# Gate products on VectorE and another layout of the conversion turns in an attention, gating and mixing kernel

## The chip, the cores and the metric

The kernel runs on one core of a Trainium2 chip. A core has TensorE (matmuls; the profile shows its matmuls as PE and its weight loads as PEld), VectorE (DVE), ScalarE (ACT), GpSimd (POOL) and SyncE (SP, which here issues the DMAs). The metric is device microseconds of one execution. All inputs lie in HBM at the start; the host only lays data out.

## The reference

Three layers follow each other, for 8 batches of 576 tokens and 512 channels.

```python
q_s = softmax(q, over the 64 channels of a head); k_s = softmax(k, over the tokens)
x = q_s @ (k_s.T @ v)                          # 8 heads, joined to 512 channels
h = gelu_tanh(x @ w_in)                        # 512 -> 1024
u, v = h[..., :512], h[..., 512:]
v_n = (v - mean(v)) / sqrt(var(v) + 1e-6) * g_ln
v_s = einsum('ts,bsd->btd', w_sg, v_n) + b_sg[None, :, None]
x = x + (u * v_s) @ w_out
u = x + (U, V applied over the tokens: low rank 32)
out = u + relu(u @ w_ch1) @ w_ch2              # 512 -> 2048 -> 512
```

w_in, w_out, U, V, w_ch1 and w_ch2 arrive as 64-bit floats, and the kernel turns them into 32-bit ones itself. Every matmul operand is split into a high and a low part, and three products (high x high, high x low, low x high) make one.

## The kernel before

**First part, batch by batch (b = 0 to 7).** TensorE's program order is written out by hand throughout; in the batches VectorE's is too, while ScalarE, GpSimd and SyncE get theirs from a planner that fills them by its own estimates. For one batch TensorE does, in this order: the v half of the hidden layer (`emit_Vh`, tiles pv, five token tiles t), the u half (`emit_Uh`, pu, four blocks f), the mixing over tokens (`emit_S`, pS, four blocks f), the key-value product of the next batch (pk), the output layer (`emit_y`, py, four column blocks c) with the transposes of the next batch's q between, and the next batch's x (`emit_xT`, px). Transposes of y and the low rank products of a batch lie between the pv tiles of the next one.

In the S stage each block f is treated as follows. VectorE reads the finished pS and makes gt = pS * gl + bb (line 658). A product gt = gt * u follows (the gate product, line 661): on POOL for blocks 0, 1 and 2, on VectorE for block 3, in every batch. `split_G` then has ScalarE copy gt to gh (the high part) and VectorE subtract to give gl (the low part); it is called for block f - 1 after `emit_S` of block f. TensorE's py needs gh and gl of all four blocks. Before the S stage's work VectorE and POOL do the division of the next batch's q by its sums (`q_norm`, tiles qt<-qt,qs): token tiles 0 and 1 on VectorE, 2, 3 and 4 on POOL.

**Conversion turns.** The channel weights w_ch1 and w_ch2 are converted in the shadow of the batches. A list `chan` holds 176 items: for each of 16 sets four Blocks (load 256 columns of 64-bit words, clamp on POOL, exponent on ScalarE, two integer instructions on VectorE at lines 179 and 180) and then seven Factors, of Block sums and differences for a seven-product scheme, numbered a = 4, 1, 5, 2, 6, 7, 3. A Factor's sum (`merge`, tile f<-f,f) is done for a = 5, 6, 7 and 3; then follow a copy on ScalarE and a subtract on POOL (chw), and SyncE stores the result to HBM (wd<-chw). `more(n)` makes n turns; a turn advances this pipeline by one item, each item being loaded, clamped, started, merged, copied, split and stored in turns of its own (a store comes 7 turns after the item is loaded, a split 5). There are 183 turns in all. In `side["add"]` stands which engine does the sums: POOL for all of them in batches 1 to 6; in batch 7 and after it VectorE for a = 5 and 7.

How many turns come where is written in the tuple `spread[b]`: after each tile of pv, each block of pu, each block of pS, and ahead of each block of py. Batches 1 to 6 have 15 turns each, the last 37. Batch 0 converts the other weights.

**Second part, 280 steps.** After the batches, tokens are taken in five groups (512, 512, 512, 384, 384 columns). A group has 56 steps: 28 that make hidden tiles h from the input u (r = 0 to 27, matmuls mm<-uh,wu and mm<-ul,wu; for the first seven the tile is called pm), then 28 that make the output (mm<-oh,wu and mm<-ol,wu). A step uses one weight tile wu, fetched from wd by SyncE into a ring of five. The first seven steps lie in the last batch, with `more` between them; `u_first` (prep) makes their operands on ScalarE and VectorE in the last batch's u and S stages. From step 7 on the order on ScalarE, VectorE, POOL and SyncE is written by hand too. In each step SyncE's fetch comes first, then the turns that are left, then `h_prep` (oh and ol three steps ahead, by ScalarE and VectorE), VectorE's sums of h (h<-h,h), POOL's sums of the next group's operand (`u_sum`, ust<-ust), and then the matmuls and what VectorE and ScalarE do with the result. The next operand's four loads (ust<-u2d, 512 KB each) are issued in step r = 7. In the first group, where POOL is busy with turns, the four `u_sum`s come at r = 29, 31, 33 and 35 (line 910); in the other groups at 12, 14, 16 and 18. When the last turn is made, the staging memory is closed and the memory for oh and ol opened in its place.

```python
tt(pool if f < NF - 1 else dve, gt, gt, u_t[b][:, f], ALU.mult)      # line 661
add = side["add"][self.a in (6, 3)]                                  # line 344
more(min(left(), 3 - (s % 4 == 0)))                                  # line 1348
```

Of the kernel before, what the change touches and what calls it, by code (L numbers as in the profile page):

```python
# [12 lines left out]
ALU = mybir.AluOpType  # L13
# [9 lines left out]
def fused_kernel(tc, q, k, v, w_in, g_ln, w_sgT, b_sg, w_out, U, V, w_ch1, w_ch2, outT):  # L23
    nc = tc.nc
    B, S, C = q.shape
# [6 lines left out]
    NF = F // P  # L32
# [9 lines left out]
    ORDER = (1, 2, 6, 7, 5, 4, 3)  # L42
# [8 lines left out]
    def tt(eng, out, a, b, op):  # L51
        return eng.tensor_tensor(out=out, in0=a, in1=b, op=op)  # L52
# [246 lines left out]
            cols = slice(h * HS, (h + 1) * HS)  # L299
            yield ConvV(V[:, cols], lambda o=v_w[:, cols]: o, eng)  # L300

    side = {"add": (pool, pool), "low": pool}
    chw = [((stgp, 4),), 0]

    class Block(Conv):
# [23 lines left out]
    class Factor(Block):  # L329
# [11 lines left out]

        def merge(self):
            w = self.keep
            add = side["add"][self.a in (6, 3)]
            if self.a == 5:
                tt(add, w[22], w[21], w[22], ALU.add)
            elif self.a == 6:
                tt(add, w[22], w[22], w[11], ALU.subtract)
            elif self.a == 7:
                tt(add, w[21], w[11], w[21], ALU.subtract)  # L350
            elif self.a == 3:
                tt(add, w[12], w[12], w[22], ALU.subtract)
            self.t = w[{1: 11, 2: 12, 3: 12, 4: 22, 5: 22, 6: 22, 7: 21}[self.a]]
# [110 lines left out]
    def q_norm(b, t, eng=pool):  # L464
        n = TR[t]
        tt(eng, q3(t), q3(t), q_s[b][0:n, t].unsqueeze(2).to_broadcast([n, H, D]), ALU.mult)
# [161 lines left out]
    u_t = {}  # L628
# [13 lines left out]
    def emit_S(b, f):  # L642
        if f == 0:
            g_t[b] = (
                wrk.tile([P, NF, S], F32R, tag="xgh", name="gh"),
                wrk.tile([P, NF, S], F32R, tag="xgl", name="gl2"),
            )
        pS = ps2.tile([P, 2, 512], F32, tag="big", name="pS")
        fs = slice(f * P, (f + 1) * P)
        for t in range(NT):  # L650
            h, l = vh[b, t]
            prod(pS, h[:, fs], l[:, fs], sg_h[:, t], sg_l[:, t], t == 0, False)
        e = vh[b, NT]
        for i, w in enumerate((sg_a, sg_b)):
            for j in range(2):
                mm(pS[:, j, 0:HS], e[:, fs], w[:, j * HS : (j + 1) * HS], False, i == 1)
        gt = tmpp.tile([P, S], F32, tag="gt", name="gt")
        dve.scalar_tensor_tensor(
            out=two(gt), in0=halves(pS), scalar=gl[:, f : f + 1], in1=two(bb), op0=ALU.mult, op1=ALU.add
        )  # L660
        tt(pool if f < NF - 1 else dve, gt, gt, u_t[b][:, f], ALU.mult)
        g_t[b, f] = gt

    def split_G(b, f):
# [237 lines left out]
    def u_side(g, r):  # L902

        n = GROUPS[g]
        if r == 7:
            us[0] = p2["ust"].tile([P, 2, 2, 2, NM], F32, tag="ust", name="ust")
            for h in range(2):
                for j in range(2):
                    u_fetch(g, h, j)
        x = r - 17 * (g == 1)  # L910
        if x in U_SUMS:
            u_sum(U_SUMS[x], n)
        r -= half_steps
        if r in U_HIGH:
            a = U_HIGH[r]
            uc[g, a] = [u_tile(x, a) for x in ("uh", "ul")]
            copy(uc[g, a][0][:, :, 0:n], u_at(*U_AT[a], n))
        if r in U_LOW:
            a = U_LOW[r]
            hi, lo = (x[:, :, 0:n] for x in uc[g, a])  # L920
            low(dve, lo, u_at(*U_AT[a], n), hi)
            if a in (6, 4, 5):
                sent.append(lambda: u_fetch(g, *U_AT[a]))
# [134 lines left out]
    def left():  # L1058
        return len(chan) + LATER[0][1] - at[0]
# [37 lines left out]

    RING = 5
    OPS = 4
    mid = ((0, 0, 0, 0, 0), (0, 0, 0, 0), (0, 2, 3, 3), (3, 3, 1, 0))  # L1100
    spread = [mid] * B
    spread[0] = ((2, 2, 1, 1, 1), (2, 1, 2, 1), (2, 2, 2, 1), (1, 1, 1, 0))
    spread[B - 1] = ((2, 2, 2, 2, 2), (3, 2, 2, 2), (2, 2, 2, 1), (3, 3, 3, 2))
    pieces.extend(conv_w_in(F, pool))
    pieces.extend(conv_w_in(F + CW, pool))
    pieces.extend(conv_w_in(0, pool))
# [65 lines left out]
    for b in range(B):  # L1172
# [37 lines left out]
        if nxt:  # L1210
            k_max(nxt)
        else:
            side["add"] = (dve, pool)
            close_wiv()
            closers = []

            def pool2(key, *args, **kw):
                p2[key], close = opened(key, *args, **kw)
                closers.append(close)

            pool2("uc", side="right")
            prep = u_first()
# [22 lines left out]
        if nxt:  # L1245
            for t in range(NT + 1):
                q_exp(nxt, t)
            k_exp(nxt)
            for t in range(NT + 1):
                q_sum(nxt, t)  # L1250
            q_total(nxt)
            for t in range(NT + 1):
                q_norm(nxt, t, dve if t < 2 else pool)

        if not nxt:
            close_wiu()
# [43 lines left out]
        else:  # L1300
            close_wo()

            def step(s):
                fetch(s + RING)
                products(s)
                after(s)
                more((1, 1, 1, 1, 2, 2, 2)[s])

            step(0)
            step(1)  # L1310
# [32 lines left out]
    for s in range(len(ORDER), len(steps)):  # L1343
# [1 line left out]
        r = s - g * PER  # L1345
        fetch(s + RING)
        if left():
            more(min(left(), 3 - (s % 4 == 0)))
            if not left():
                close_stgp()  # L1350
                close_cst()
                pool2("ops", side="left")
# [61 lines left out]
```

## Time and profile before

| | us |
|---|---|
| median of 3 runs | 1360.58 |
| lowest and highest | 1359.35, 1360.96 |
| the profiled execution's own time | 1359.37 |
| its span | 1357.6 |
| PE busy | 1278.7 (94%) |
| DVE busy | 993.0 (73%) |
| ACT busy | 663.3 (49%) |
| POOL busy | 433.6 (32%) |

The span is the time from the first instruction to the last. A share of busy time is a mean over parts with different limits, so the rows below are read by stretch. The granted clock (PEclk) is a share of TensorE's 2.4 GHz; over the span it was 0.986.

### The profile page before, as it was taken

Reading aid. Unit: us, or ns where it says so; the run is one execution under the profiler, and the core shown is the slowest. Engines: PE = TensorE matmul, PEld = TensorE weight load, DVE = VectorE, ACT = ScalarE, POOL = GpSimd, SP = SyncE. Lnnn points to the kernel's source line nnn. Section 1 sums busy time; section 2 is a strip of 40 time slices with the busy share of each in tenths; the row PEclk is TensorE's granted clock in tenths of the full one; section 3 lists DMA queues with packets and bytes.
Section 4 is the critical chain, followed back from the end, with each engine's and each line's share of the span. In section 5 each row is a group of like instructions: output and inputs, shape, how many; then the busy total and the mean of one; then the engine's idle time right before and its main releaser. Section 6 shows DMA issues by size and latency. Waiting matters only on the chain.

```text
span 1357.6 us, 20699 instructions
## 1 busy us (share of the span) xinstructions
PE 1278.7 (94%) x7576; PEld 1140.9 (84%) x7576; DVE 993.0 (73%) x1376; ACT 663.3 (49%) x1001; POOL 433.6 (32%) x505
## 2 busy tenths in 40 slices
PE   4579999989999999998998999999999999999998
PEld 2478898979898988887776888888888889999998
DVE  7867868877787777579768974489546974695585
ACT  3774657566666656564445442345224432352342
POOL 4945364663545564466355001100020002000000
PEclk9889999999999999998999999999999999999999
DMA  7513334360616171266897687668776789889786
GB/s 237 164 48 97 105 107 127 110 194 31 178 55 177 60 229 36 94 198 232 294 409 271 220 289 268 197 218 286 242 244 204 242 273 307 264 300 325 258 282 221
DMA packets 136213, 274.68 MB, mean 202 GB/s; under 512 B 15280, under 2 KB 56752, under 8 KB 136112
## 3 DMA queue, kind: packets, MB, share of 16 engines
q1 hardware_dynamic: 136112, 273.37, 60.9%
q8 instruction: 60, 0.98, 0.3%
q14 instruction: 41, 0.34, 0.1%
HBM read 225.09 MB, written 48.23 MB: 201 GB/s over the span
## 4 chain that ended last, share of the span: by engine, by line
PE 68%; DVE 12%; DMA 7%; ACT 6%; issue 3%; POOL 3%; SPq 1%; DVEq 0%; ACTq 0%; POOLq 0%
PE mm L49 46%; PE py L49 5%; PE pu L49 4%; PE pS L49 4%; PE pv L49 3%; DMA wu<-wd 3%; DMA wd<-chw 2%; DVE f L179 1%; DVE km L52 1%; DVE yt L52 1%; DVE bst L603 1%; PE pm L49 1%; PE pt L520 1%; PE px L49 1%; DVE ul L52 1%
## 5 line engine op out<-in xcount | busy, mean ns | idle before, releaser
L49 PE MATMUL mm<-oh,wu 128*128 128x512 f32 (+1 forms) x1120 | 321.8, 368 | 1.7 <-ACT oh L58 1.7
L49 PE MATMUL mm<-uh,wu 128*128 128x512 f32 (+1 forms) x1064 | 305.1, 368 | 5.1 <-DMA wu<-wd 3.6
L49 PEld LDWEIGHTS mm<-oh,wu 128*128 128x128 f32 x1120 | 207.6, 188 | 28.4 <-ACT oh L58 2.2
L49 PEld LDWEIGHTS mm<-uh,wu 128*128 128x128 f32 x1064 | 196.6, 188 | 31.8 <-issue 4.1
L49 PE MATMUL mm<-ol,wu 128*128 128x512 f32 (+1 forms) x560 | 206.6, 369 | 2.5 <-DVE ol L52 2.5
L49 PE MATMUL mm<-ul,wu 128*128 128x512 f32 (+1 forms) x532 | 195.4, 367 | 0.0
L58 ACT ACTIVATE oh<-h 128x1024 fp32r<-128x1024 f32 (+1 forms) x140 | 132.8, 971 | 103.9 <-PE mm L49 99.4
L52 DVE TENSOR_TENSOR ol<-h,oh 128x1024 fp32r<-128x1024 f32 (+1 forms) x140 | 158.0, 1128 | 27.1 <-ACT oh L58 27.0
L1004 ACT ACTIVATE h<-h 128x1024 f32<-128x1024 f32 (+1 forms) x80 | 77.7, 972 | 174.2 <-DVE h L52 174.2
L52 POOL TENSOR_TENSOR ust<-ust 128x1024 f32<-128x1024 f32 (+1 forms) x16 | 35.7, 2239 | 391.7 <-DMA ust<-u2d 250.4
L52 DVE TENSOR_TENSOR h<-mm,u 128x1024 f32<-128x1024 f32 (+1 forms) x76 | 84.4, 1110 | 100.3 <-PE mm L49 97.1
L49 PEld LDWEIGHTS mm<-ol,wu 128*128 128x128 f32 x560 | 105.5, 188 | 17.4 <-DVE ol L52 4.2
L49 PEld LDWEIGHTS mm<-ul,wu 128*128 128x128 f32 x532 | 100.2, 188 | 12.3
L52 POOL TENSOR_TENSOR chw<-f,chw 128x256 fp32r<-128x256 f32 x112 | 87.0, 791 | 58.6 <-ACT chw L58 58.6
L52 DVE TENSOR_TENSOR u<-mm,u 128x1024 f32<-128x1024 f32 (+1 forms) x72 | 79.8, 1108 | 30.8 <-PE mm L49 30.6
L52 DVE TENSOR_TENSOR h<-h,h 128x1024 f32<-128x1024 f32 (+1 forms) x80 | 91.5, 1144 | 0.9 <-ACT h L1004 0.9
L58 ACT ACTIVATE chw<-f 128x256 fp32r<-128x256 f32 x112 | 42.7, 412 | 73.4 <-DVE f L180 27.2
L58 ACT ACTIVATE u<-mm 128x1024 f32<-128x1024 f32 (+1 forms) x24 | 22.5, 937 | 112.0 <-PE mm L49 84.5
L167 POOL TENSOR_SCALAR stg<-stg 128x256 f32<-128x256 f32 (+2 forms) x91 | 46.4, 513 | 55.4 <-DMA stg<-in_w_ch_dram 32.5
L49 PE MATMUL py<-gh,wo_h 128*128 128x288 f32 x256 | 57.6, 307 | 4.6 <-DVE yt L52 2.0
L49 PE MATMUL py<-gl,wo_h 128*128 128x288 f32 x256 | 55.8, 300 | 5.7 <-DVE gl L52 5.7
L49 PE MATMUL pu<-xh,wih 128*128 128x288 f32 x256 | 57.7, 308 | 2.2 <-DVE ge L52 1.5
(162 smaller groups left out, 2692.3 us busy)
## 6 DMA issues: line engine op xcount, KB each, us to landing
wu<-wd SPq DMA_DIRECT2D x280, 512.0 KB, 4.4
wd<-chw SPq DMA_DIRECT2D x112, 256.0 KB, 3.9
stg<-in_w_ch_dram SPq DMA_DIRECT2D x64, 256.0 KB, 3.0
u2d<-yt SPq DMA_DIRECT2D x32, 288.0 KB, 2.3
vt<-in_v_dram SPq DMA_DIRECT2D x32, 256.0 KB, 6.5
qt<-in_q_dram SPq DMA_DIRECT2D x7, 1024.0 KB, 6.8
kt<-in_k_dram SPq DMA_DIRECT2D x7, 1024.0 KB, 6.3
ust<-u2d SPq DMA_DIRECT2D x14, 512.0 KB, 6.3
```

Of the source, the lines that this page charges most:

```text
L49: pe.matmul(out, lhsT, rhs, start=first, stop=last)
L52: return eng.tensor_tensor(out=out, in0=a, in1=b, op=op)
L58: return act.activation(out, src, AF.Copy)
L167: eng.tensor_scalar(out=hi, in0=hi, scalar1=F64_MOST, scalar2=-F64_MOST, op0=ALU.min, op1=ALU.max)
L179: dve.tensor_scalar(out=b, in0=b, scalar1=3, scalar2=None, op0=ALU.logical_shift_left)
L520: pe.transpose(pt[:, t * P : t * P + n], qt[0:n, t, c * P : (c + 1) * P], ident[0:n, 0:n])
L603: dve.bn_stats(out=bst[0:n], in_=ge[0:n])
L1004: act.activation(h, h, AF.Relu)
```

## The change

Five edits are made. The gate product is made by VectorE for blocks 0, 1 and 3 in batches 1 to 6 and for all blocks in batch 7; batch 0 keeps its places. The block sum of a = 5 goes to VectorE in all batches. One q_norm tile (t = 1) goes from VectorE to POOL in batches 1 to 6. The four POOL sums for the second group come at r = 21, 23, 25 and 27. And the turns are laid out anew: batches 1 to 6 have 15, 15, 15, 15, 14 and 16 turns, the last 36, the first seven steps 11 instead of 10; the 46 that are left are taken by the tuple FIRST from step 7 on, and end at step 25, where they ended at step 23.

```diff
-    side = {"add": (pool, pool), "low": pool}
+    side = {"add": {5: dve}, "low": pool}
...
-            add = side["add"][self.a in (6, 3)]
+            add = side["add"].get(self.a, pool)
...
-        tt(pool if f < NF - 1 else dve, gt, gt, u_t[b][:, f], ALU.mult)
+        tt(pool if (f < NF - 1 if b == 0 else f == 2 and b < B - 1) else dve, gt, gt, u_t[b][:, f], ALU.mult)
...
-        x = r - 17 * (g == 1)
+        x = r - 9 * (g == 1)
...
-    mid = ((0, 0, 0, 0, 0), (0, 0, 0, 0), (0, 2, 3, 3), (3, 3, 1, 0))
-    spread = [mid] * B
+    vh0, uh0 = (0, 0, 0, 0, 0), (0, 0, 0, 0)
+    spread = [
+        None,
+        ((1, 0, 0, 0, 0), uh0, (0, 2, 3, 2), (2, 4, 1, 0)),
+        (vh0, (1, 0, 0, 0), (0, 2, 3, 3), (3, 2, 1, 0)),
+        (vh0, (0, 0, 1, 0), (0, 2, 3, 3), (2, 3, 1, 0)),
+        (vh0, uh0, (0, 2, 3, 3), (3, 3, 1, 0)),
+        (vh0, (0, 0, 0, 1), (0, 1, 3, 2), (2, 3, 1, 1)),
+        (vh0, (0, 0, 0, 1), (0, 1, 4, 3), (3, 2, 1, 1)),
+        ((2, 2, 2, 3, 2), (3, 1, 1, 3), (2, 1, 2, 0), (4, 3, 3, 2)),
+    ]
+    FIRST = (2, 2, 3, 2, 2, 3, 3, 3, 2, 3, 3, 3, 1, 3, 4, 2, 1, 2, 3, 3)
     spread[0] = ((2, 2, 1, 1, 1), (2, 1, 2, 1), (2, 2, 2, 1), (1, 1, 1, 0))
-    spread[B - 1] = ((2, 2, 2, 2, 2), (3, 2, 2, 2), (2, 2, 2, 1), (3, 3, 3, 2))
...
-            side["add"] = (dve, pool)
+            side["add"] = {5: dve, 7: dve}
...
-                q_norm(nxt, t, dve if t < 2 else pool)
+                q_norm(nxt, t, dve if t < (1 if b else 2) else pool)
...
-                more((1, 1, 1, 1, 2, 2, 2)[s])
+                more((2, 2, 2, 1, 0, 3, 1)[s])
...
-            more(min(left(), 3 - (s % 4 == 0)))
+            x = s - len(ORDER)
+            more(min(left(), FIRST[x] if x < len(FIRST) else 3))
```

## Rows read from the trace of the kernel before

The stretches of rows 1 are batches 1, 2, 5 and 6 (pu to pu), the last y stage, steps 0 to 6, 7 to 12, 13 to 27, 28 to 31, and 24 later steps; behind the engines stand the granted clock, the DMA share and GB/s.

**Rows 1.** Busy time of each engine in stretches: length, then PE, PEld, DVE, ACT, POOL

```profile
153.87:224.01 70.14, 69.79 (x528) 64.61 (x527) 53.75 (x100) 44.13 (x72) 34.62 (x41) 1.00 0.37 114
224.01:299.23 75.22, 71.15 (x529) 64.44 (x528) 58.72 (x104) 47.48 (x83) 44.46 (x54) 1.00 0.43 137
...
441.20:515.22 74.02, 70.58 (x528) 64.48 (x527) 56.91 (x102) 47.22 (x83) 44.21 (x53) 1.00 0.43 135
515.22:587.99 72.77, 70.50 (x526) 63.99 (x524) 49.67 (x97) 45.22 (x75) 38.40 (x46) 1.00 0.25 83
...
617.33:638.63 21.30, 15.58 (x98) 14.76 (x97) 20.95 (x31) 9.04 (x19) 10.90 (x12) 0.84 0.77 265
638.63:666.52 27.89, 25.51 (x124) 20.34 (x122) 22.75 (x35) 13.55 (x26) 11.31 (x16) 1.00 0.81 261
666.52:687.12 20.60, 18.25 (x72) 14.64 (x73) 11.12 (x19) 6.32 (x14) 9.39 (x13) 0.92 1.01 364
687.12:730.84 43.72, 42.06 (x182) 33.45 (x180) 35.39 (x44) 23.87 (x43) 31.41 (x39) 1.00 1.00 378
730.84:749.02 18.18, 13.94 (x50) 9.74 (x49) 16.11 (x14) 6.97 (x7) 4.04 (x2) 0.91 0.47 174
749.02:814.30 65.28, 65.28 (x290) 54.05 (x289) 55.69 (x49) 29.64 (x29) 0.00 (x0) 1.00 0.77 264
```

**Rows 2.** Waits of PE from 140 to 588 us: total, times, longest

```profile
PE pv L49 <- POOL xl L52: 2.8, 3, 1.9
```

**Rows 3.** Timeline of PE, last y stage: start, us, instruction, idle before it

```profile
622.43 0.85 PE L49 MATMUL py<-gl,wo_h 128*128 128x288 f32 x2 [3.55 <-DVE gl L52]
626.34 0.85 PE L49 MATMUL py<-gl,wo_h 128*128 128x288 f32 x2 [2.11 <-DVE gl L52]
```

**Rows 4.** Timeline of PE where step 12 begins

```profile
682.76 0.70 PE L49 MATMUL mm<-uh,wu 128*128 128x512 f32 x2 [2.35 <-DMA wu<-wd]
```

**Rows 5.** Gate products: duration in ns (min, median, max), first and last start

```profile
L52 POOL TENSOR_TENSOR gt<-gt,ut x24: 1412/1427/1933, 102.5 to 619.3; 128x576 f32<-128x576 f32 x24
L52 DVE TENSOR_TENSOR gt<-gt,ut x8: 757/759/1159, 114.9 to 624.5; 128x576 f32<-128x576 f32 x8
```

**Rows 6.** The q_norm of VectorE, same columns

```profile
L52 DVE TENSOR_TENSOR qt<-qt,qs x19: 631/674/896, 24.2 to 534.5; 128x512 f32<-128x512 f32 x18, 64x512 f32<-64x512 f32 x1
```

**Rows 7.** Timeline of POOL, S stage of batch 4

```profile
388.16 4.19 POOL L52 TENSOR_TENSOR qt<-qt,qs 128x512 f32<-128x512 f32 x3 [10.98 <-ACT kt L432]
```

**Rows 8.** Timeline of DVE, S stage of batch 4

```profile
394.49 1.25 DVE L52 TENSOR_TENSOR gl<-gt,gh 128x576 fp32r<-128x576 f32 x1 [1.85 <-ACT gh L58]
```

**Rows 9.** Timeline of POOL at its sums for the second group

```profile
723.31 11.57 POOL L52 TENSOR_TENSOR ust<-ust 128x1024 f32<-128x1024 f32 x4
```

**Rows 10.** Timeline of DVE during these sums and after them

```profile
723.46 3.33 DVE L52 TENSOR_TENSOR h<-h,h 128x1024 f32<-128x1024 f32 x1 [0.89 <-ACT h L1004]
...
729.18 3.44 DVE L52 TENSOR_TENSOR ol<-h,oh 128x1024 fp32r<-128x1024 f32 x1
...
735.93 1.21 DVE L52 TENSOR_TENSOR h<-h,h 128x1024 f32<-128x1024 f32 x1
```

**Rows 11.** Block sums of Factors, columns as in rows 5

```profile
L52 POOL TENSOR_TENSOR f<-f,f x49: 726/737/1239, 190.1 to 720.3; 128x256 f32<-128x256 f32 x49
...
L52 DVE TENSOR_TENSOR f<-f,f x15: 411/497/959, 596.6 to 717.9; 128x256 f32<-128x256 f32 x15
```

**Rows 12.** Timeline of POOL, S stage of the last batch

```profile
610.00 2.51 POOL L52 TENSOR_TENSOR f<-f,f 128x256 f32<-128x256 f32 x2
...
613.62 1.43 POOL L52 TENSOR_TENSOR gt<-gt,ut 128x576 f32<-128x576 f32 x1
```

**Rows 13.** Timeline of DVE, S stage of the last batch

```profile
615.81 1.95 DVE L52 TENSOR_TENSOR gl<-gt,gh 128x576 fp32r<-128x576 f32 x1 [2.74 <-ACT gh L58]
```

**Rows 14.** Timeline of SP, step 7: issues

```profile
671.15 2.32 SPq L889 DMA_DIRECT2D ust<-u2d  x4
673.86 0.98 SPq L761 DMA_DIRECT2D wu<-wd  x2
```

## The prediction

> **What bounds the kernel now.** I read the table of stretches first. A stretch is compared with its kind at full pace, and what it is longer by is all that a change of order can win, because the number of matmuls stays the same. TensorE is busy for all but fractions of a microsecond in the best of the middle batches: batch 1 takes 70.14 us [rows 1]. Batches 2, 5 and 6 take 75.22, 74.02 and 72.77, so 5.1, 3.9 and 2.6 are lost there; batches 3 and 4 lie between, with little to win. The y stage of the last batch is 21.30 long with 15.58 of TensorE, at 0.84 of the clock. In the steps that follow, 24 undisturbed ones take 65.28, so one step is 2.72. Steps 7 to 12 take 20.60 instead of 16.3 (4.3 lost), steps 13 to 27 take 43.72 instead of 40.8 (2.9), steps 28 to 31 take 18.18 instead of 10.9 (7.3) [rows 1]. Steps 0 to 6 with what lies between them are 27.89 with 25.51 of TensorE (2.4). Together with about 8 of the y stage (5.7 of idle, and the halved clock) that is some 36 us that could be won; everything else is TensorE at its pace.
>
> Then the waits, stretch by stretch, for what ends last. In the middle batches it is POOL's low part of x, 2.8 us in 3 waits [rows 2]; the reader is to see that the two long batches are those with 44.46 and 44.21 us of POOL work, against 34.62 in the shortest [rows 1]. In the last y stage TensorE waits 3.55 and 2.11 us for VectorE's gl [rows 3]. At step 12 it is a fetch that lands late [rows 4]; at steps 28 to 31 the high and low operands, which VectorE makes in its order.
>
> **The change part by part.** Durations are those of the profiled execution (1359.37 us; the median of the runs is 1.2 above it), and the sum is made against it.
>
> *Gate products of batches 1 to 6.* Two of the three POOL products (1.427 us each) go to VectorE, where one takes 0.759 [rows 5]; one q_norm goes the other way, 0.674 on VectorE, and 4.19/3 = 1.4 on POOL [rows 6, 7]. On VectorE that adds 2 x 0.759 - 0.674 = 0.8 us a batch. The cover is the wait for gh in the same stage: VectorE stands 1.85 us before the first gl [rows 8], because POOL makes three q_norms before the two gates [rows 7]; with the gate made by VectorE this wait goes, and what is late next is the scalar product of block 2, which VectorE then reaches at about the same time. Without that cover it would be 0.8 x 6 = 5 us later. TensorE has no wait in this stage, so I take 0, between -2 and +5.
>
> Work of two engines on the same memory shows: an h sum of VectorE takes 3.33 us while POOL runs its sums and 1.21 after them [rows 9, 10]. The Trainium skill, SBUF — State Buffer, section Who interferes with whom, says that a VectorE instruction with two SBUF inputs and a GpSimd instruction that reads SBUF exclude each other for a whole instruction. By that rule each moved gate also waits for the q_norm running beside it, so VectorE would be some 1 us later in each of the batches, which speaks against this part; rows 10 agree with the rule.
>
> *POOL's load in those batches.* It loses 2 x 1.427 for gates and 1.3 block sums of 0.737 [rows 5, 11] (16 sets of 11 items; 90 turns in six batches are 8 sets), and gains 1.4: net -2.4 us a batch. Batches 2 and 5 against batch 1 give 4.5 us of length for 9.7 us of POOL [rows 1], 0.46 us for each, so 1.1 us in each of the three long batches: -3.3. Turns: batch 5 has 7 instead of 9 before its first y add, batch 3 has 8; batch 6 has 10. For this I add -1.7, an estimate of a seventh of the 11.6 lost in the three long batches. The block sum adds 0.497 [rows 11] to VectorE 1.3 times a batch, which lies beside TensorE's py. I take -5; the bounds are -10 (nearly all that is lost) and +5 (one more batch like batch 2, since each batch now meets another phase of the 11 items).
>
> *Last batch.* All gates go to VectorE. Now POOL reaches gate 0 at 613.62 only after two block sums that took 2.51 us [rows 12], and VectorE stands 2.74 us for the first gl, which then takes 1.95 [rows 13], while it has the second block's work behind it. After: three products more (2.3 us), less that wait, less one turn ahead of the last gl, and the first gl no longer runs beside POOL's gate (up to 1.2 us). VectorE should reach the last gl 2 to 3 us earlier, and TensorE stands that much less before its 626.34 [rows 3]. With a part of the halved clock that is -3.5; bounds 0 (VectorE fills the time with other work, being busy 20.95 of 21.30 us [rows 1]) and -8.
>
> *Steps 0 to 6.* 11 turns instead of 10, and 6 instead of 3 in the first three steps, where VectorE also owes the y adds. VectorE has 22.75 of 27.89 us to do there [rows 1]. I take +1; bounds -2.4 and +3.
>
> *Steps 7 to 27.* The turns left are 46, as before. They were 3 or 2 a step and ended at step 23; now they are 2 to 4, and end at step 25. In steps 7 to 12 the fetch for step 12 is issued 2.7 us behind four loads of the next operand (671.15) and lands after TensorE has come to it; TensorE waits 2.35 us and then runs at 0.92 of the clock [rows 1, 4, 14]. 11 turns instead of 14 in steps 7 to 11 put fewer loads and stores into SP's queue around these; but the four loads stay. -1, bounds -4.3 and +2. For steps 13 to 27 I take 0, bounds -2.9 and +4: two steps more with conversions, and three POOL sums between them. SP's stores wait for POOL's low parts, and the fetches stand behind the stores.
>
> *The four sums for the second group.* They moved from steps 29 to 35 to steps 21 to 27 in POOL's order. POOL ran them in one piece, 11.57 us from 723.31 [rows 9], as soon as its conversions were done, and in this piece an h sum took 3.33 and an operand's low part 3.44 us instead of 1.21 [rows 10]: 4.35 us on VectorE, just ahead of the operands for steps 28 to 31. Spread over seven steps three of the four come before that; the last can still meet it: 3/4 of 4.35, or 3.3, so -3.5 with what the halved clock (0.91 in that stretch [rows 1]) gives back; bounds -7.3 and 0.
>
> **Sum:** 0 - 5 - 3.5 + 1 - 1 + 0 - 3.5 = -12, so 1347.4 profiled, and 1348.6 for the runs with the 1.2 between them; I say 1348.5.
>
> **Rivals.** *The middle batches give nothing* (1353.5). Their lost time then does not come from POOL's load but from VectorE's order; the turns and the sums that VectorE gets keep it late. For: x's low part is only 2.8 us of the waits [rows 2]; against: the lengths follow POOL's load [rows 1]. Faster still.
>
> *The gains cancel* (1360). VectorE is the bound of the last y stage (20.95 of 21.30), so the gates cost what the wait gives; the sums slow VectorE in steps 21 to 27 as much as they did later. Then the terms of the last batch and of the sums are 0, the middle gives a little, and the first steps take it. For: VectorE's 35.39 of 43.72 us in steps 13 to 27 [rows 1]. Against: that leaves it 8 us of idle time, and 4.35 are disputed.
>
> *Slower* (1367). The three sums at steps 21, 23 and 25 stand in POOL's queue between conversions whose results SP stores; SP holds the fetches of the weights behind these stores. Each sum is 2.9 us; where the fetch lands with nothing to spare, as it did at step 12 [rows 4], TensorE waits for each: 8.7 us, the sums' gain is lost, and the middle batches give nothing: -3.5 + 1 + 8.7 = +6.2. It decides once POOL falls behind its conversions by more than the ring of five weight tiles covers. For: the stores do wait for POOL. Against: POOL is idle 12.3 us of the 43.72 [rows 1], about what the sums take.
>
> **How the numbers follow.** My forecast gets 0.52, the middle giving nothing 0.20, cancelling 0.11, slower 0.17. Faster by over 0.2% (2.7 us, about what a measurement of this kernel can tell from no change) is then 0.72, within it 0.11, slower 0.17. The likeliest case alone reaches from 1338 to 1354. The range goes from 1335 (the middle and the sums near their better bounds) to 1362, past the cancelling case; about 0.1 of the slower case lies beyond, and some of the better one below.
>
> **What would show it.** Batches 2 and 5 nearer 72 us; the wait for gl in the last y stage under 4 us in all, and no idle time of VectorE before the first gl; steps 28 to 31 in 14 to 15 us, with h sums at 1.2 us there; POOL's sums as four pieces between conversions. Wrong would be: fetch waits in steps 21 to 27, batches of 74 us in other places, or a last y stage of 21 us again.

## The result, and the profile after

| | before | after |
|---|---|---|
| median of the runs, us | 1360.77 (4 runs) | 1345.40 (4 runs) |
| lowest and highest | 1359.35, 1361.32 | 1344.43, 1345.79 |
| the profiled execution, us | 1359.37 | 1344.43 |
| its span | 1357.6 | 1342.7 |

The changed kernel is faster: the ratio of the times is 0.989, with a 95% interval from 0.987 to 0.9905. The forecast was 1348.5. Against the profiled execution of before, where the sum was made, it was -12, and -14.9 came.

The table of stretches comes first, cut at the same points of the program as [rows 1]. Length, then busy time of PE, PEld, DVE, ACT and POOL; behind them the granted clock, the DMA share and GB/s. The stretches of the changed kernel are batches 1 to 6 one by one, then steps 0 to 6, 7 to 12, 13 to 27 and 28 to 31.

```profile
153.77:223.92 70.15, 69.80 (x529) 64.60 (x528) 54.76 (x102) 43.91 (x72) 32.70 (x39) 1.00 0.39 114
223.92:294.12 70.20, 69.85 (x529) 64.61 (x528) 58.82 (x106) 44.66 (x74) 38.62 (x43) 1.00 0.41 128
294.12:365.06 70.94, 70.27 (x528) 64.54 (x527) 55.39 (x101) 47.32 (x81) 38.27 (x46) 1.00 0.42 126
365.06:436.83 71.77, 70.50 (x530) 64.51 (x528) 57.55 (x104) 43.87 (x72) 33.62 (x40) 1.00 0.38 116
436.83:507.43 70.60, 70.01 (x527) 64.60 (x527) 57.18 (x104) 44.51 (x74) 36.01 (x42) 1.00 0.40 123
507.43:580.83 73.40, 70.45 (x524) 64.05 (x523) 54.68 (x101) 49.16 (x86) 44.60 (x53) 1.00 0.30 103
...
627.34:654.62 27.28, 25.60 (x123) 20.24 (x121) 24.31 (x39) 13.45 (x26) 12.83 (x19) 1.00 0.83 279
654.62:672.87 18.25, 16.71 (x73) 13.55 (x74) 9.06 (x14) 4.47 (x9) 6.89 (x10) 1.00 1.02 369
672.87:716.90 44.03, 41.62 (x181) 33.55 (x180) 35.72 (x45) 25.40 (x48) 32.28 (x41) 1.00 1.02 380
716.90:734.30 17.40, 13.42 (x49) 9.87 (x48) 13.99 (x13) 6.97 (x7) 4.86 (x2) 0.90 0.61 212
```

The reader is to see that the long batches 2 and 5 [rows 1] are gone (70.20 and 70.60), that batch 6 is the only long one left, and that in the second part only steps 7 to 12 moved by more than a microsecond. Set side by side, with the stages merged where a cut between them falls differently in two profiles:

| stage | before | after | change | forecast |
|---|---|---|---|---|
| batches 1 to 6 | 434.12 | 427.06 | -7.1 | -5 |
| last batch, its pu to step 0 | 50.64 | 46.51 | -4.1 | -3.5 |
| steps 0 to 6 | 27.89 | 27.28 | -0.6 | +1 |
| steps 7 to 12 | 20.60 | 18.25 | -2.4 | -1 |
| steps 13 to 27 | 43.72 | 44.03 | +0.3 | 0 |
| steps 28 to 31 | 18.18 | 17.40 | -0.8 | -3.5 |
| all after step 31 | 608.57 | 608.35 | -0.2 | |

The total is near, but the split is not: the middle gave more and steps 28 to 31 gave nearly nothing. Their 0.8 us is less than the scatter: the kernel before and two others that are as before from step 7 on took 18.18, 16.44 and 17.17 us there, and the changed kernel and five others that are like it from step 7 on took 16.63 to 19.36. The waits of TensorE in the middle (140 to 590 us of the changed kernel; total, times, longest) no longer name POOL, which ended the most waiting in [rows 2]:

```profile
PE pv L49 <- ACT ge L593: 1.8, 6, 0.5
PE pu L49 <- DVE ge L52: 1.4, 1, 1.4
PE pw L49 <- DVE yt L52: 1.0, 1, 1.0
```

In the last y stage of the changed kernel the two waits of [rows 3] are shorter (timeline of PE: start, us, instruction, idle before it),

```profile
612.11 0.53 PE L49 MATMUL py<-gl,wo_h 128*128 128x288 f32 x2 [0.88 <-DVE gl L52]
614.97 0.85 PE L49 MATMUL py<-gl,wo_h 128*128 128x288 f32 x2 [1.79 <-DVE gl L52]
```

and VectorE no longer stands before the first gl, which takes 0.75 us where it took 1.95 after a wait of 2.74 [rows 13] (timeline of DVE, S stage of the last batch):

```profile
600.23 1.12 DVE L52 TENSOR_TENSOR gt<-gt,ut 128x576 f32<-128x576 f32 x1
...
607.22 0.75 DVE L52 TENSOR_TENSOR gl<-gt,gh 128x576 fp32r<-128x576 f32 x1
```

The four sums of POOL come in three pieces in the changed kernel, the last two sums back to back:

```profile
704.96 2.59 POOL L52 TENSOR_TENSOR ust<-ust 128x1024 f32<-128x1024 f32 x1
...
711.28 3.41 POOL L52 TENSOR_TENSOR ust<-ust 128x1024 f32<-128x1024 f32 x1
...
716.05 5.71 POOL L52 TENSOR_TENSOR ust<-ust 128x1024 f32<-128x1024 f32 x2
```

VectorE's low parts and h sums there, two of which took 3.33 and 3.44 us [rows 10], now take 1.74 to 2.07. But a wait stands before one of them (timeline of DVE, changed kernel, up to step 29):

```profile
710.67 1.75 DVE L52 TENSOR_TENSOR h<-h,h 128x1024 f32<-128x1024 f32 x1 [1.71 <-ACT h L1004]
...
715.42 1.74 DVE L52 TENSOR_TENSOR ol<-h,oh 128x1024 fp32r<-128x1024 f32 x1 [0.55 <-POOL chw L52]
...
720.77 2.07 DVE L52 TENSOR_TENSOR ol<-h,oh 128x1024 fp32r<-128x1024 f32 x1 [1.33 <-DMA wu<-wd]
```

TensorE stands for that low part (timeline of PE, changed kernel):

```profile
722.89 0.50 PE L49 MATMUL mm<-ol,wu 128*128 128x512 f32 x1 [2.65 <-DVE ol L52]
```

A low part made from h and oh needs no weight tile, so "wu<-wd" can't be what it waits for. The DMAs that end just before 720.77 are the last two stores of converted weights, issued at 715.42 and 716.11 and landed at 719.83 and 720.45. Whether these are the cause was tried below.

### The profile page after: what moved, and what is told of

Its sections match the earlier page's. It is cut to its first block, busy times and chain, and to the rows that moved or that the text cites. A ratio compares the mean times of both kernels' runs of the same rounds, so it can differ in the third digit from the quotient of the medians.

```text
span 1342.7 us, 20693 instructions
## 1 busy us (share of the span) xinstructions
PE 1274.2 (95%) x7576; PEld 1139.7 (85%) x7576; DVE 1002.7 (75%) x1393; ACT 662.7 (49%) x1001; POOL 420.1 (31%) x488
## 4 chain that ended last, share of the span: by engine, by line
PE 71%; DVE 13%; DMA 6%; ACT 4%; issue 3%; POOL 2%; SPq 1%; DVEq 0%; ACTq 0%; POOLq 0%
PE mm L49 46%; PE pu L49 5%; PE py L49 5%; PE pS L49 5%; PE pv L49 4%; DMA wu<-wd 2%; DVE f L179 1%; PE px L49 1%; DMA qt<-in_q_dram 1%; POOL chw L52 1%; DVE km L52 1%; DVE yt L52 1%; DVE f L180 1%; PE pp L49 1%; PE pt L692 1%
## 5 line engine op out<-in xcount | busy, mean ns | idle before, releaser
L52 POOL TENSOR_TENSOR chw<-f,chw 128x256 fp32r<-128x256 f32 x112 | 91.9, 837 | 50.1 <-ACT chw L58 47.2
```

## Experiments: the middle batches

All are made from the changed kernel unless the text says otherwise, and each was timed beside the kernel before on its chip. The times of the six batches are those of one profile each. How far they can be trusted shows from kernels whose edits leave these batches alone: seven with the batches of the changed kernel took 425.9 to 427.2 us in them, two with those of before 434.1 and 434.2.

**The gates back on POOL** (batches 1 to 6 alone).

```diff
-        tt(pool if (f < NF - 1 if b == 0 else f == 2 and b < B - 1) else dve, gt, gt, u_t[b][:, f], ALU.mult)
+        tt(pool if (f < NF - 1 if b < B - 1 else False) else dve, gt, gt, u_t[b][:, f], ALU.mult)
```

> The changed kernel, with the gate products of blocks 0 and 1 of batches 1 to 6 back on POOL; all else as changed. Theory A (the two long middle batches were set by POOL's load): POOL gets 2.85 us a batch more, so the batches with most POOL work grow by 1 to 2 us each, about 4 us in all: 1349 us. Theory B (the layout of the turns took the time out, the gates were covered): within 1.5 us of the changed kernel's 1345.4, and the lengths of batches 2 and 5 stay near 70.5.

Measured: 1351.24, ratio to the kernel before 0.994 [0.992, 0.995]. The six batches took 432.59, so 5.5 of the 7.1 us are lost again. Its runs reach from 1348.89 to 1353.89 and the profiled one took 1353.32, so the 5.5 may be on the high side. TensorE's waits there have other names than before (waits of PE, 140 to 590 us):

```profile
PE py L49 <- DVE ql L52: 3.3, 2, 2.1
...
PE py L49 <- DVE yt L52: 1.4, 1, 1.4
```

It now waits for VectorE, and VectorE is late because it stands for POOL's gates. Timeline of DVE in the S stage of batch 6, gates on POOL:

```profile
535.50 1.25 DVE L52 TENSOR_TENSOR gl<-gt,gh 128x576 fp32r<-128x576 f32 x1 [3.23 <-ACT gh L58]
```

The same first low part in the changed kernel:

```profile
531.00 0.96 DVE L52 TENSOR_TENSOR gl<-gt,gh 128x576 fp32r<-128x576 f32 x1 [0.56 <-ACT gh L58]
```

So the cover that the prediction named (VectorE's wait for gh) is there, and its removal is worth time on the path, where the prediction had put 0.

**The gates alone**, added to the kernel before.

```diff
-        tt(pool if f < NF - 1 else dve, gt, gt, u_t[b][:, f], ALU.mult)
+        tt(pool if (f < NF - 1 if b in (0, B - 1) else f == 2) else dve, gt, gt, u_t[b][:, f], ALU.mult)
```

> The kernel before, with the gate products of blocks 0 and 1 of batches 1 to 6 alone moved from POOL to VectorE. Theory A: the six batches come from 434.1 to about 429 us, and the kernel to 1354. Rival B (it takes the new layout of the turns as well): under 2 us of gain, 1358.

Measured: 1353.84, ratio 0.9955 [0.994, 0.997]. The six batches took 429.92: 4.2 of the 7.1 us come from this line alone. The wait for POOL's low part of x is shorter too, where it was 2.8 us in [rows 2] (waits of PE, 140 to 590 us, gates alone):

```profile
PE pv L49 <- POOL xl L52: 0.9, 2, 0.5
```

So a part of the 4.2 us is POOL's relief, and not VectorE's wait for POOL's gates.

**The block sum of a = 5 back on POOL** (batches 1 to 6).

```diff
-    side = {"add": {5: dve}, "low": pool}
+    side = {"add": {}, "low": pool}
```

> The changed kernel, with the block sum of a = 5 back on POOL in batches 1 to 6. Theory A with the slope of the prediction (0.46 us of length for 1 us of POOL): POOL gets 1 us a batch, so 1 to 2 us over all, 1347. Theory K (only the wait of VectorE behind POOL's gates counted, and POOL's other load does not): within 1 us of 1345.4, the six batches together at 427 as now.

Measured: 1350.64, ratio 0.9935 [0.992, 0.995]. The six batches took 432.66, so this one edit holds 5.6 us (the profiled execution, 1352.74, was the longest of its runs). The waits of PE for POOL's low part of x come back as in [rows 2]:

```profile
PE pv L49 <- POOL xl L52: 2.2, 3, 1.2
```

The edit moves nine sums between pu of batch 1 and pu of the last (POOL makes 34 there instead of 25), but it moves more than these. The later sums of a set need the one of a = 5. VectorE's order is written by hand, so in the changed kernel that sum of the second set of batch 2 stands at its turn, in the S stage of batch 3 (317.76 us), and three more sums and five splits (chw) come behind it on POOL. With the sum on POOL, the planner ran all of this ahead of its turns, between 268 and 280 us, around the low parts of x (timeline of POOL, x stage of batch 2, sum on POOL):

```profile
274.03 1.43 POOL L52 TENSOR_TENSOR xl<-x,xh 128x576 fp32r<-128x576 f32 x1
275.41 0.75 POOL L52 TENSOR_TENSOR f<-f,f 128x256 f32<-128x256 f32 x1
276.11 1.44 POOL L52 TENSOR_TENSOR xl<-x,xh 128x576 fp32r<-128x576 f32 x1
```

In the changed kernel the two low parts there run in one piece:

```profile
273.30 2.83 POOL L52 TENSOR_TENSOR xl<-x,xh 128x576 fp32r<-128x576 f32 x2 [3.67 <-PE pt L692]
```

Batch 5 shows the same. With the sum on POOL, as before the change, batches 2 and 5 have 14 splits and 8 sums of POOL each; in the changed kernel they have 9 and 3, and batches 3 and 6 go from 7 and 9 splits to 12 and 16. (Batch 6, the one long batch left, has the work that left batch 5.) The 5.6 us lie in these two batches: they take 72.36 and 75.33 us for 70.20 and 70.60, and the other four together 1.3 us less. So what counts is what the sum takes along, and not its own 0.74 us.

**One q_norm tile back on VectorE.**

```diff
-                q_norm(nxt, t, dve if t < (1 if b else 2) else pool)
+                q_norm(nxt, t, dve if t < 2 else pool)
```

> The changed kernel, with the second q_norm tile of batches 1 to 6 back on VectorE. Theory A (POOL's load sets the long batches): POOL is 1.4 us lighter, 1 to 3 us faster over the six batches: 1343 to 1344. Theory L (VectorE's order sets them): VectorE gets 0.7 us a batch in front of the gates, 1 to 3 us slower: 1347 to 1348. Neither: within 1 us.

Measured: 1345.17, ratio 0.9896 [0.988, 0.991], six batches 426.42. No difference from the changed kernel.

**The turns of batches 1 to 6 as they were.**

```diff
+    mid = ((0, 0, 0, 0, 0), (0, 0, 0, 0), (0, 2, 3, 3), (3, 3, 1, 0))
+    spread[1:7] = [mid] * 6
```

> The changed kernel, with the turns of batches 1 to 6 back in the old places (0, 2, 3, 3 in S and 3, 3, 1, 0 ahead of y in every batch, 90 turns in all as before). Theory A (POOL's load): the relief of POOL stays, so at most 2 us come back: 1345 to 1347. Theory B (the layout): most of the 7.1 us that the middle batches lost comes back, batches 2 and 5 near 74 again: 1350 to 1352.

Measured: 1346.96, ratio 0.9905 [0.989, 0.992], six batches 426.64 against 427.06. The new layout of the turns in these batches is worth nothing that can be measured here: beside the gates and the sum, the old one does as well.

The six batches in one row each (same columns as above): before,

```profile
153.87:587.99 434.12, 422.20 (x3160) 386.48 (x3159) 327.34 (x598) 272.46 (x452) 231.44 (x271) 1.00 0.37 116
```

the changed kernel,

```profile
153.77:580.83 427.06, 420.89 (x3159) 386.90 (x3158) 338.40 (x613) 273.44 (x454) 223.80 (x258) 1.00 0.38 118
```

the block sum back on POOL,

```profile
154.37:587.03 432.66, 422.80 (x3159) 386.47 (x3159) 328.95 (x604) 271.60 (x452) 223.77 (x265) 1.00 0.37 116
```

and the gates alone.

```profile
153.59:583.51 429.92, 422.05 (x3160) 386.51 (x3159) 333.64 (x610) 271.96 (x452) 218.50 (x259) 1.00 0.37 117
```

The last two show that the prediction's yardstick, 0.46 us of length for each us of POOL's load, does not hold. With the block sum on POOL its busy time is that of the changed kernel (223.77 and 223.80), and the batches are 5.6 us longer. With the gates alone POOL has the least to do of all four (218.50), and they are 2.9 us longer. What counts is in which batch and in which place of POOL's order the work stands. The two edits aren't additive either: each undone by itself costs most of the gain (5.5 and 5.6, together 11.1 of 7.1), and yet the gates alone give 4.2. With the sum on POOL the q_norm tile and the new turns together cost 2.7 us (432.66 against 429.92), while with the sum on VectorE each of them is worth nothing. Gates on POOL hold VectorE up, the sum on POOL holds x's low part up, and either is enough to make TensorE late.

## Experiments: the last batch

**Its gates alone**, added to the kernel before.

```diff
-        tt(pool if f < NF - 1 else dve, gt, gt, u_t[b][:, f], ALU.mult)
+        tt(pool if f < NF - 1 and b < B - 1 else dve, gt, gt, u_t[b][:, f], ALU.mult)
```

> The kernel before, with the three gate products of the last batch alone moved from POOL to VectorE. Theory E (VectorE's wait for POOL's gates set the last y stage): the two waits for gl shrink from 5.7 to under 3.5 us and the stage from 21.3 to about 18: 3 us faster, 1357.5. Rival F (VectorE is full, and the fewer turns in that stage did it): within 1 us of before, waits for gl still over 5 us.

Measured: 1356.13, ratio 0.998 [0.997, 0.9985]. From pu of the last batch to step 0 it took 49.28 instead of 50.64. VectorE's wait before the first gl is gone, as expected, but TensorE's two waits are as long as in [rows 3] (timeline of PE, gates alone):

```profile
619.46 0.54 PE L49 MATMUL py<-gl,wo_h 128*128 128x288 f32 x2 [3.02 <-DVE gl L52]
623.51 0.85 PE L49 MATMUL py<-gl,wo_h 128*128 128x288 f32 x2 [2.99 <-DVE gl L52]
```

**The last batch's turns as they were**, with the gates of the changed kernel.

```diff
-        ((2, 2, 2, 3, 2), (3, 1, 1, 3), (2, 1, 2, 0), (4, 3, 3, 2)),
+        ((2, 2, 2, 2, 2), (3, 2, 2, 2), (2, 2, 2, 1), (3, 3, 3, 2)),
...
-                more((2, 2, 2, 1, 0, 3, 1)[s])
+                more((1, 1, 1, 1, 2, 2, 2)[s])
```

> The changed kernel, with the last batch's turns back (10, 9, 7, 11 and 10 in the first seven steps, 47 in all as now). Moving the gates alone took only 1.4 us off the S and y stages of the last batch together (50.6 to 49.3), the whole change 4.1 (46.5). Theory G (the turns ahead of the gates hold the rest, since VectorE is full there): these stages come to 48.5 to 49.5, the kernel to about 1348. Rival H (gates and a run's clock made it all): under 47.3, 1345.5.

Measured: 1347.31, ratio 0.991 [0.989, 0.993]; the stage took 47.58, where the kernels with the new layout in this batch take 46.2 to 47.5. The two waits (timeline of PE, old layout in the last batch):

```profile
611.67 0.53 PE L49 MATMUL py<-gl,wo_h 128*128 128x288 f32 x2 [1.45 <-DVE gl L52]
615.72 0.85 PE L49 MATMUL py<-gl,wo_h 128*128 128x288 f32 x2 [2.99 <-DVE gl L52]
```

Turns and gates of the last batch are the same in these two kernels, and still one takes 1.7 us longer than the other; what they enter the stage with differs. So a part of the 4.1 us may be handed on from the batches before; with one profile each, where kernels with the same last batch lie up to 1.3 us apart, that is not shown. The second wait goes with the layout: it is 2.99 us in both kernels with the old one, and 1.71 to 1.79 in the changed kernel and in eight others of this study with the new one (in the ninth, with the middle gates on POOL, TensorE came to it later and waited 0.26). That is 1.2 us of this wait for the layout, most likely for the two turns fewer between the blocks of pS; in the length of the stage the layout is not told apart from the scatter. How the rest of the 4.1 us divides between the gates and what is handed on stays open; the pieces are as small as the scatter between profiles.

## Experiments: steps 7 to 35

**The four sums back at r = 29 to 35.**

```diff
-        x = r - 9 * (g == 1)
+        x = r - 17 * (g == 1)
```

> The changed kernel, with POOL's four sums for the second group back at r = 29 to 35. Theory C (the sums slow VectorE just ahead of steps 28 to 31, as the prediction had it): steps 28 to 31 get 2 to 4 us longer than 17.4, 1348 us. Theory D (steps 28 to 31 wait for the memory under the operands' low parts, which is free only when the last conversion's store has landed): without sums between them the last conversions end some 4 us earlier, the wait of 2.65 us at step 29 goes, and the kernel is as fast as changed or up to 2 us faster: 1343 to 1346.

Measured: 1346.03, ratio 0.990 [0.989, 0.9915]. POOL does the sums in one piece again (710.47, 11.53 us), and VectorE's h sum beside it takes 3.39 us, with the same wait before the low part (timeline of DVE, sums back):

```profile
717.46 2.31 DVE L52 TENSOR_TENSOR ol<-h,oh 128x1024 fp32r<-128x1024 f32 x1 [1.24 <-DMA wu<-wd]
719.70 3.39 DVE L52 TENSOR_TENSOR h<-h,h 128x1024 f32<-128x1024 f32 x1
```

The stretches of steps 7 to 27 and 28 to 31 of this kernel:

```profile
652.25:714.55 62.30, 58.35 (x253) 47.10 (x254) 44.28 (x60) 29.87 (x56) 37.52 (x50) 1.00 1.02 379
714.55:734.86 20.31, 15.15 (x49) 10.92 (x48) 17.00 (x13) 6.96 (x7) 7.37 (x3) 0.83 0.46 174
```

Steps 28 to 31 take 20.31 against 17.40 with the sums early: 2.9 us, near the 3.3 that was worked out for the contention, with a part of it through the clock (0.83 for 0.90). But the five other kernels with the sums early took 16.63 to 19.36 there, so the difference is between 0.9 and 3.7 us. That the sums slow VectorE is seen; that this is worth 3.3 us is not shown. Over the whole run the kernels are not told apart (1346.03 and 1345.40): batch 4 and steps 0 to 6 of this profile came out 1.3 us shorter each, the last batch 1.0 longer. Since against before only 0.8 us were won in steps 28 to 31, something that came with the change takes the rest there.

**The turns after step 7 as they were** (they end at step 23; the POOL sums stay at r = 21 to 27).

```diff
-            more(min(left(), FIRST[x] if x < len(FIRST) else 3))
+            more(min(left(), 3 - (s % 4 == 0)))
```

> The changed kernel, with the turns after step 7 back at 3 or 2 a step, so that they end at step 23; POOL's sums stay at r = 21 to 27. Theory D (step 29 waits for the memory under its low operand, free when the last store has landed): the store comes two steps sooner, the wait of 2.65 us at step 29 is gone or under 0.5, and steps 28 to 31 take 14 to 16 instead of 17.4 us. Steps 7 to 12 with 14 instead of 11 turns in the first five: the prediction's step says the wait at step 12 is longer again, 19 to 20.5 us instead of 18.2. In all within 2 us of 1345.4. Rival: steps 28 to 31 stay at 17 to 18, because VectorE is behind in any case.

Measured: 1348.13, ratio 0.991 [0.990, 0.993]. No wait stands before the low parts of steps 28 and 29, but with POOL free earlier three sums run in one piece (711.90, 8.10 us), and the low part falls into it (timeline of DVE, turns to step 23):

```profile
717.78 3.29 DVE L52 TENSOR_TENSOR ol<-h,oh 128x1024 fp32r<-128x1024 f32 x1
```

Steps 28 to 31 took 17.85, and steps 13 to 27 46.55 where they had taken 44.03. Steps 7 to 12 took 18.34, not the 19 to 20.5 that was expected, with a wait of 1.62 us for the fetch of step 12 against 1.54: the turns after step 7 are not what made this stretch shorter. This kernel has two causes in one place and can't part them; the last experiment below takes one of them away.

**The next operand's loads moved out of step 7** to r = 30, and its sums with them (r = 36 to 42), still on POOL.

```diff
-        if r == 7:
+        if r == (30 if g == 1 else 7):
...
-        x = r - 9 * (g == 1)
+        x = r - 24 * (g == 1)
```

> The changed kernel, with the second group's four operand loads (2 MB) issued in step 30 instead of step 7, and POOL's sums of them at r = 36 to 42. Theory I (the four loads hold up the fetch of step 12, and the sums slow VectorE ahead of step 28): steps 7 to 12 take 16.4 to 17 instead of 18.2, steps 28 to 31 take 15 to 16 instead of 17.4, the kernel comes to 1341.5. Rival J (the sums then slow VectorE in steps 33 to 38, where it is busy 85% of the time): these steps lose 2 to 5 us, and the kernel stays at 1345 or above.

Measured: 1345.75, ratio 0.990 [0.988, 0.9915]: the total did not move. But two stretches did, in opposite directions. Steps 7 to 27, 28 to 31, and the 65.28 us behind them in this kernel:

```profile
653.32:710.57 57.25, 57.25 (x253) 47.42 (x253) 43.95 (x61) 30.55 (x57) 33.69 (x48) 1.00 1.02 374
710.57:726.32 15.75, 12.04 (x50) 8.70 (x49) 11.16 (x11) 6.46 (x7) 0.00 (x0) 1.00 0.91 347
726.32:791.60 65.28, 60.68 (x259) 49.22 (x258) 61.59 (x49) 29.52 (x29) 12.54 (x4) 0.97 0.68 242
```

TensorE is busy for all of the 57.25 us of steps 7 to 27, 21 steps at 2.73, where the changed kernel needs 62.28. It is the loads and not the sums: with the sums alone put back behind these steps (above; only their first 4 us still ran in them) the stretch took 62.30. So the four loads cost 5.0 us there. In the changed kernel TensorE waits three times for a fetch in these steps (2.5 us in all); in this one, never. They are given back in steps 32 to 38, because the sums now run where VectorE has no idle time (last row: TensorE 60.68 of 65.28 us instead of 65.28). POOL and DVE, same kernel:

```profile
726.75 12.70 POOL L52 TENSOR_TENSOR ust<-ust 128x1024 f32<-128x1024 f32 x4 [20.14 <-DMA ust<-u2d]
```

```profile
727.18 3.42 DVE L52 TENSOR_TENSOR ol<-h,oh 128x1024 fp32r<-128x1024 f32 x1
730.52 3.40 DVE L52 TENSOR_TENSOR h<-h,h 128x1024 f32<-128x1024 f32 x1
733.85 3.35 DVE L52 TENSOR_TENSOR ol<-h,oh 128x1024 fp32r<-128x1024 f32 x1
```

Three instructions in a row take 3.4 us instead of 1.2, and TensorE waits 4.6 us for low parts.

**The same with the four sums on VectorE** in the second group.

```diff
-    def u_sum(a, n):
+    def u_sum(a, n, eng):
...
-            u_sum(U_SUMS[x], n)
+            u_sum(U_SUMS[x], n, dve if g == 1 else pool)
```

> The changed kernel, with the second group's operand loads in step 30 (as in the run before with late loads) and its four sums made by VectorE at r = 36, 38, 40 and 42 instead of by POOL. Theory J (POOL's sums slowed VectorE there from 1.22 to 3.4 us an instruction, and that ate what the late loads gave): steps 7 to 27 stay at full pace (57.2 us), steps after 32 lose 0 to 2 us instead of 7.5, and the kernel comes to 1338 to 1341, faster than both. Rival (VectorE has no room for four sums of 1.2 us there either): the steps after 32 lose 4 us or more, 1343 or above.

Measured: 1338.61, ratio 0.985 [0.983, 0.986], faster than the changed kernel. The sums cost VectorE 1.22 us each, and everything after step 31 takes 609.45 again instead of 616.05. Beside POOL the three instructions shown cost more (6.5 us over their time alone) than the four whole sums do on VectorE (4.9).

One wait is left in steps 28 to 31, with no POOL sum near (timeline of DVE, sums on VectorE):

```profile
713.60 1.23 DVE L52 TENSOR_TENSOR ol<-h,oh 128x1024 fp32r<-128x1024 f32 x1 [2.20 <-DMA wu<-wd]
```

The last store of converted weights landed at 713.48 here. In all eight kernels of this study that have this wait, it ends 0.12 to 0.32 us after that landing.

**And the turns ending at step 23.** This kernel differs from the last one only in the line of the turns, the edit that also put them back above. Oh and ol are laid into the staging memory of the conversions, which is free when the last store has read it; if that store is what the low part waits for, the wait must go when the turns end two steps earlier.

```diff
-            more(min(left(), FIRST[x] if x < len(FIRST) else 3))
+            more(min(left(), 3 - (s % 4 == 0)))
```

> The kernel with late loads and VectorE's sums, and with the turns after step 7 back at 3 or 2 a step, so that they end at step 23. POOL has no sums there, so only the memory under oh and ol is left to tell. Theory D (the operand of step 29 waits for the last conversion's store): VectorE's wait of some 2.5 us before its second low operand is gone, steps 28 to 31 take 13 to 15 instead of 17.2 us; steps 7 to 27 lose at most 2 us to the denser turns; 1336 to 1338. Rival (VectorE is behind at the turn from hidden to output steps in any case): steps 28 to 31 stay at 16.5 to 18, and the kernel is not faster than 1338.6.

Measured: 1337.40, ratio 0.984 [0.9825, 0.985]. The wait is gone (timeline of DVE, turns to step 23, sums on VectorE),

```profile
712.52 1.22 DVE L52 TENSOR_TENSOR ol<-h,oh 128x1024 fp32r<-128x1024 f32 x1
```

and steps 28 to 31 take 12.88 us (steps 7 to 27, then 28 to 31):

```profile
654.18:712.29 58.11, 57.63 (x252) 47.25 (x253) 45.03 (x61) 30.68 (x57) 33.58 (x48) 1.00 1.01 370
712.29:725.17 12.88, 11.47 (x49) 8.85 (x48) 10.81 (x11) 6.19 (x7) 0.00 (x0) 1.00 0.96 362
```

With the turns to step 25 they took 17.17 with 13.70 of TensorE. Now there are 2.1 us less of idle time, and 2.2 less of TensorE's busy time, since the clock is not halved behind the wait (0.90 and 1.00). The last store landed at 710.37, 2.15 us before the low part starts. So the wait that came into steps 28 to 31 with the change is the one for the staging memory. Of the 4.3 us, 3.8 are seen in the span (1337.28 and 1333.52). The medians lie 1.2 us apart with intervals that overlap, so the runs as a whole do not show this kernel faster than the one before it; that it is faster than the changed kernel, they do. Memory of its own for the Factors' tiles, which would take the wait away without touching the turns, did not fit, so it has no time.

## Why the prediction was near, and which steps failed

**What bounds the kernel: right.** The time came from the stretches that the table of [rows 1] showed longer than their kind, and the rest stayed: all after step 31 is within 0.2 us.

**Gates of the middle batches, taken at 0: too small.** They give 4.2 us alone, a part of it by POOL's relief, which the prediction has in its next term. The prediction saw that VectorE stood for POOL's gates [rows 8] and that the wait would go, but set it to nothing because TensorE showed no wait in the S stage. VectorE's lateness is carried on: with the gates on POOL, TensorE waits in the y stage, for ql and yt. The fear that the moved gates would collide with the q_norm beside them came true only in part, at a size that did not matter. This is the same tile's list of durations as [rows 5], for the changed kernel:

```profile
L52 DVE TENSOR_TENSOR gt<-gt,ut x23: 757/845/1292, 114.1 to 613.5; 128x576 f32<-128x576 f32 x23
```

VectorE's median rose by 0.09 us from 0.759, and the slowest took 1.29. The Trainium skill, SBUF — State Buffer, section Who interferes with whom, has the one that issues first hold the shared ports for its whole instruction while the other is blocked. For a gate behind a q_norm that would be up to 1.6 us by the q_norm's median here, and no gate lost more than 0.53. The first moved gate of a batch started just before a q_norm and lost nothing (0.757 to 0.760 us in all six batches); it was that q_norm that took 1.55 us, where it took 1.04 with the gates on POOL.

**POOL's load (-3.3) and the turns (-1.7): the sum came out, the working failed.** The load's yardstick was read from three batches that differed in more than POOL's load; two kernels with the same load or less disprove it. The turns gave 0. What was right is that POOL's late x was the bound in batches 2 and 5. But the prediction had the block sum as 0.737 us of load [rows 11], for which the yardstick gives 3.1 us (9 x 0.737 x 0.46), and never as what the rest of its set waits for; putting it back costs 5.6 us, because the rest of two sets comes back into the x stages of batches 2 and 5. The rival in which VectorE's order keeps the middle batches late is half true: VectorE was the second cause.

**Last batch, -3.5: right** at -4.1, by the mechanism as far as VectorE's wait goes. But the gates alone leave TensorE's waits as they were: VectorE fills the time with other work, which the prediction had as the bound at 0, and it needed the rest of the change.

**Steps 0 to 27: right within their bounds.** Steps 0 to 6 did not get longer (-0.6 for +1). In steps 7 to 12 TensorE's busy time fell from 18.25 to 16.71 because the halved clock is gone (1.00 for 0.92), which is 1.5 of the 2.4 us; the rest is shorter waits. The step that the prediction gave for it, 11 turns instead of 14 in steps 7 to 11, did not make them so: with the old turns after step 7 the stretch took 18.34 us, and with the old ones in the last batch and the first seven steps 17.84. What did stays open. The clock can be luck: the kernel with only the last batch's gates moved is the same as before from step 7 on, and had it at 1.00 there. The slower rival did not come: in the steps with sums between the conversions one fetch was waited for, 0.60 us. After, steps 7 to 27 have the DMA share at 1.02, and their remaining 5 us are the four loads of 512 KB.

**Steps 28 to 31, -3.5: failed** at -0.8. The step that failed is that the operands for steps 28 to 31 come 3.3 us earlier once POOL's sums no longer slow VectorE's two instructions ahead of them. They are slowed much less (1.74 to 2.07 us for 3.33 and 3.44), but with the turns ending at step 25 instead of 23 a new wait came: the oh and ol tiles lie in the memory that the last conversions' stores still read. The prediction counted the two steps more against the fetches and never against the memory that is opened when the last turn is made, though that was in the kernel to be read. Without that wait, and without POOL's sums, the stretch takes 12.88 us; the forecast had 14 to 15.

That the total was near is luck in part, because these two misses have opposite signs: 2.1 us too little in the middle and 2.7 too much at steps 28 to 31, and the smaller terms came out 3.5 us better. The two faster kernels show what the change left: with the loads out of step 7, the sums on VectorE and the turns ending at step 23, the kernel runs at 1337.4. Batch 6, the last y stage and steps 0 to 6 are still longer than their kind.

## What to carry to other kernels

Where an engine stands for another engine's work in a stage in which TensorE does not wait, look at what that engine is late with in the next stage before the gain is set to nothing. Before a stream of work is stretched by some steps, look up which memory is handed over when it ends, and who writes there first: such a wait shows under the name of a DMA that the tile has nothing to do with. And before work is moved to an idle engine, look at what stands beside it: four sums that cost VectorE 4.9 us cost it more when POOL did them. And an instruction that is moved to an engine with an order written by hand also fixes when all that needs it can run: that, and not its length, was what the block sum was worth.

## What the runs showed of the hardware

A VectorE instruction of two SBUF inputs (128x1024) takes 1.21 us alone and 3.3 to 3.4 us for as long as POOL's sums run (12.70 us for four). In steps 7 to 27 of the changed kernel the DMA share is 1.02 at 369 to 380 GB/s; the 2 MB of the next operand, loaded in that stretch, cost 5 us. The share alone does not show this: it was 1.02 as well with the loads moved out, where TensorE never waited. And a stretch in which TensorE runs at 1.2 instead of 2.4 GHz follows a wait of a few microseconds in some executions and not in others. The kernel before and the one with only the last batch's gates moved are the same from step 7 on: in steps 7 to 12 one had a wait of 2.35 us, a granted clock of 0.92 and 18.25 us of TensorE, the other a wait of 2.90 us, a clock of 1.00 and 16.97. So a stretch of 20 us can differ by over a microsecond between two profiles for that alone.
